# Merging two layers' attention loops of neighbouring batch elements in a decode kernel

## The chip, the cores and the metric

The kernel runs on one core of a Trainium2 chip. The metric is the device time of one execution in microseconds (us). *Slow* is a run over 1.5% above the fastest of the same kernel, and only *fast* runs enter the ratios.

Names used below: PE is the matmul engine (TensorE) and PEld its weight load, DVE is VectorE, ACT is ScalarE, POOL is GpSimd. "Issue" in the profile is time in which an engine waited for nothing that the profile shows. A "q spread" is the small group of PE matmuls that spreads a query out before its scores; it marks the same place in every element. A "packet" is one record of a DMA transfer in the trace.

## The reference

Two transformer-like layers with the same weights and the same K/V cache, one after the other: 4 batch elements, one token each, 32 query heads on 8 K/V heads, 4096 cached positions of 128 values, all bf16.

```python
B, Sq, D = 4, 1, 512;  Hq, Hkv, Sk, Dh = 32, 8, 4096, 128;  F = 1792   # cut
def _A_ref(x, k_cache, v_cache, wq, wo):
    q = (x @ wq).reshape(B, Sq, Hq, Dh)                    # transposes cut
    scores = einsum("bhqd,bhkd->bhqk", q, k) * Dh ** -0.5
    p = softmax(scores)
    return einsum("bhqk,bhkd->bhqd", p, v).reshape(B, Sq, Hq * Dh) @ wo
def _B_ref(x, w_gate, w_up, w_down):
    return (gelu(x @ w_gate) * (x @ w_up)) @ w_down

x = x + _A_ref(layernorm(x), ...)
x = x + _B_ref(layernorm(x), ...)
x = x + _A_ref(layernorm(x), ...)
x = x + _B_ref(layernorm(x), ...)
```

K and V are 33.5 MB each. The kernel keeps one element's transposed K on the chip for both layers, but reads V twice, so with the weights it moves 114.6 MB.

## The kernel before

Every K or V tile is a load of 512 KB into a ring of seven buffers, all issued from one engine. An element's K, V and V again are 48 such loads.

```python
KV_BUFS = 7
def load_kv(cache, b, kvh, t, name):
    tl = kvin.tile([P, CH, Dh], BF16, name=name, tag="kv")
    src = cache[b, kvh].rearrange("(p c) d -> p c d", p=P)
    dq.dma_start(out=tl[:], in_=src[:, t * CH:(t + 1) * CH])
    return tl

def turn(b, kvh):            # load K and transpose it with VectorE
    ...
        kn = load_kv(A_k_cache, b, kvh, t, "k_t")
        ...
            nc.vector.transpose(out=kt[...], in_=kf[:, :, bb])

def scores_head(sc, s, kvh, qb):          # 32 matmuls a head
    ...
            nc.tensor.matmul(sc[:, s, g, :], lhsT=kt[:, g, be // 2, :, be % 2],
                             rhs=qb[:, be, kvh]..., ...)

def soft_a(sc):              # max, exp
    nc.vector.tensor_reduce(out=colmax[:], in_=v, axis=AX.X, op=ALU.max)
    nc.gpsimd.partition_all_reduce(gmax..., colmax..., P, RED.max)
    nc.vector.tensor_tensor(out=w, in0=w, in1=gmax..., op=ALU.subtract)
    nc.scalar.activation(out=raw..., in_=sc..., func=ACT.Exp, scale=scale)

def soft_b(raw, pool):       # the "swap": 16 small matmuls, then a copy
    ...
            nc.tensor.matmul(x[a * QS:(a + 1) * QS, :, :, cc, :],
                             lhsT=ident_bf[:, cc * QS:(cc + 1) * QS], rhs=raw[:, :, :, a, :], ...)
    nc.scalar.copy(out=pe..., in_=x...)

def soft_c(pe):              # denominators with a matmul of ones
    nc.tensor.matmul(d..., lhsT=ones_bf[:, :], rhs=pe..., start=True, stop=True)
    nc.vector.tensor_reduce(out=den[:], in_=d..., axis=AX.X, op=ALU.add)

class Values:                # one step = one load of V and its 16 matmuls
    def step(self, count=1):
        ...
            v = load_kv(A_v_cache, self.b, kvh, t, "v_t")
            for i in range(CH):
                c = t * CH + i
                nc.tensor.matmul(self.ot[:], lhsT=v[:, i, :], rhs=pe[:, s, c, :],
                                 start=(c == 0), stop=(c == C - 1))

for b in range(B):
    for g in range(NG):                      # first layer, 4 groups of 2 heads
        ... turn, scores_head, soft_a, values of the group before, soft_b, soft_c, out_proj
    ... out_proj, norm, FFN, norm, q          # filled with second-layer values of element b-1
    for g in range(NG):                      # second-layer scores, on their own
        for s in range(GH):
            scores_head(sc, s, g * GH + s, qb2)
        nxt = soft_a(sc)
        ...
    prev = Values(b, 2, prob2)               # its values fill the next element's FFN
```

Of the kernel before, what the change touches and what calls it, by code (L numbers as in the profile page):

```python
# [8 lines left out]
FP32 = mybir.dt.float32  # L9
# [6 lines left out]
P = 128  # L16
# [4 lines left out]
GH = 2  # L21
QD = 4
QS = P // QD
KV_BUFS = 7
# [3 lines left out]
def kernel(  # L28
# [27 lines left out]
    NB = 2  # L56
# [9 lines left out]
    qbp = ctx.enter_context(tc.tile_pool(name="qbp", bufs=1))  # L66
    rawp = ctx.enter_context(tc.tile_pool(name="rawp", bufs=2))
    p1p = ctx.enter_context(tc.tile_pool(name="p1p", bufs=2))
    p2p = ctx.enter_context(tc.tile_pool(name="p2p", bufs=NG + 1))
    grp = ctx.enter_context(tc.tile_pool(name="grp", bufs=2 * NG))  # L70
    small = ctx.enter_context(tc.tile_pool(name="small", bufs=1))
    ps_sc = ctx.enter_context(tc.tile_pool(name="ps_sc", bufs=2, space=bass.MemoryType.PSUM))
    ps_ot = ctx.enter_context(tc.tile_pool(name="ps_ot", bufs=1, space=bass.MemoryType.PSUM))
    ps_y = ctx.enter_context(tc.tile_pool(name="ps_y", bufs=1, space=bass.MemoryType.PSUM))
    ps_x = ctx.enter_context(tc.tile_pool(name="ps_x", bufs=2, space=bass.MemoryType.PSUM))
# [6 lines left out]
    ones_bf = const.tile([P, P], BF16, name="ones_bf")  # L82
    nc.vector.memset(ones_bf[:], 1.0)
# [18 lines left out]
    wq_dram = A_wq.rearrange("(k p) n -> p k n", p=P)  # L102

# [21 lines left out]
    def ln_stats(b0, nb):  # L125
        bs = slice(b0, b0 + nb)
        st = ps_misc.tile([P, 2, nb, KD], FP32, name="st", tag="misc")
        nc.tensor.matmul(st[:], lhsT=mean_f[:, :], rhs=XX[:, :, bs], start=True, stop=True)
        return st

    def ln_apply(b0, nb, st):
        mv = small.tile([P, 2, nb], FP32, name="mv", tag="mv")
        nc.vector.tensor_reduce(out=mv[:], in_=st[:], axis=AX.X, op=ALU.add)
        msq = small.tile([P, nb], FP32, name="msq", tag="msq")
# [17 lines left out]
        for i in range(nb):  # L152
            nc.vector.tensor_scalar(out=xn_bf[:, :, b0 + i], in0=XX[:, 0, b0 + i],  # L153
                                    scalar1=mv[:, 0, i:i + 1], scalar2=rstd[:, i:i + 1],
                                    op0=ALU.subtract, op1=ALU.mult)

    def q_proj(b0, nb, h0, hp, dst):
        bs = slice(b0, b0 + nb)
        qps = ps_misc.tile([P, hp, nb], FP32, name="qps", tag="misc")
        for i in range(hp):  # L160
            m = h0 + i
            for k in range(KD):
                nc.tensor.matmul(qps[:, i, :], lhsT=wq_sb[:, k, m * Dh:(m + 1) * Dh],  # L163
                                 rhs=xn_bf[:, k, bs], start=(k == 0), stop=(k == KD - 1))
        nc.vector.tensor_copy(out=dst, in_=qps[:])

    def q_spread(q_rows, qb, h0, hp):
        qe = ps_misc.tile([P, NB * 2, hp], FP32, name="qe", tag="misc")
        for b in range(NB):
            for e in range(2):  # L170
                nc.tensor.matmul(qe[:, b * 2 + e], lhsT=sel[:, b, e].rearrange("p a i -> p (a i)"),
                                 rhs=q_rows, start=True, stop=True)
        k0, nk = h0 // rep, hp // rep
        for be in range(NB * 2):
            nc.vector.tensor_tensor(
                out=qb[:, be, k0:k0 + nk],
                in0=qe[:, be].rearrange("p (k h) -> p k h", h=rep).unsqueeze(2)
                    .broadcast_to([P, nk, QD, rep]),
                in1=amask[:].unsqueeze(1).unsqueeze(3).broadcast_to([P, nk, QD, rep]),
                op=ALU.mult)  # L180
# [23 lines left out]
    def gelu(nb, hg):  # L204
        sq = small.tile([P, KF, nb], FP32, name="sq", tag="sq")
        nc.scalar.activation(out=sq[:], in_=hg[:], func=ACT.Square)
        nc.vector.tensor_scalar(out=sq[:], in0=sq[:], scalar1=0.044715, scalar2=1.0,
                                op0=ALU.mult, op1=ALU.add)
        nc.vector.tensor_tensor(out=sq[:], in0=sq[:], in1=hg[:], op=ALU.mult)
        th = small.tile([P, KF, nb], FP32, name="th", tag="th")  # L210
        nc.scalar.activation(out=th[:], in_=sq[:], func=ACT.Tanh, scale=GELU_C)
        nc.vector.scalar_tensor_tensor(out=th[:], in0=th[:], scalar=1.0, in1=hg[:],
                                       op0=ALU.add, op1=ALU.mult)
        return th

    def gate_up(nb, th, hu):
        H_bf = small.tile([P, KF, nb], BF16, name="H_bf", tag="H_bf")
        nc.vector.scalar_tensor_tensor(out=H_bf[:], in0=hu[:], scalar=0.5, in1=th[:],
                                       op0=ALU.mult, op1=ALU.mult)
# [13 lines left out]
    def turn(b, kvh):  # L233
        kt = ktp.tile([P, G8, NB, QD, QS], FP32, name="kt", tag="kt")
        KT[kvh] = kt
        gt = CH // QD
        for t in range(NT):
            kn = load_kv(A_k_cache, b, kvh, t, "k_t")
            kf = kn.rearrange("p c d -> p (c d)").bitcast(FP32).rearrange(
                "p (c b i) -> p c b i", b=NB, i=QS)  # L240
            for bb in range(NB):
                nc.vector.transpose(  # L242
                    out=kt[:, t * gt:(t + 1) * gt, bb].rearrange("p g c j -> p g (c j)"),
                    in_=kf[:, :, bb])

    def scores_head(sc, s, kvh, qb):
        kt = KT[kvh].rearrange("p g b c j -> p (g b c j)").bitcast(BF16).rearrange(
            "p (g b m e) -> p g b m e", b=NB, m=P, e=2)
        for g in range(G8):
            for be in range(NB * 2):  # L250
                nc.tensor.matmul(sc[:, s, g, :], lhsT=kt[:, g, be // 2, :, be % 2],  # L251
                                 rhs=qb[:, be, kvh].rearrange("p a h -> p (a h)"),
                                 start=(be == 0), stop=(be == NB * 2 - 1))
# [4 lines left out]
    def soft_a(sc):  # L258
        v = sc.rearrange("p s g (a h) -> p s h (g a)", h=rep)
        colmax = grp.tile([P, GH, rep], FP32, name="colmax", tag="colmax", bufs=2)  # L260
        nc.vector.tensor_reduce(out=colmax[:], in_=v, axis=AX.X, op=ALU.max)  # L261
        gmax = grp.tile([P, GH, rep], FP32, name="gmax", tag="gmax", bufs=2)
        nc.gpsimd.partition_all_reduce(gmax.rearrange("p s h -> p (s h)"),  # L263
                                       colmax.rearrange("p s h -> p (s h)"), P, RED.max)
        w = sc.rearrange("p s g (a h) -> p s (g a) h", h=rep)
# [8 lines left out]
    def soft_b(raw, pool):  # L274
# [12 lines left out]
    def soft_c(pe):  # L287
        d = ps_x.tile([P, GH, C, rep], FP32, name="d", tag="x")
        nc.tensor.matmul(d.rearrange("p s c h -> p (s c h)"), lhsT=ones_bf[:, :],  # L289
                         rhs=pe.rearrange("p s c h -> p (s c h)"), start=True, stop=True)  # L290
        den = grp.tile([P, GH, rep], FP32, name="den", tag="den", bufs=2)
        nc.vector.tensor_reduce(out=den[:], in_=d.rearrange("p s c h -> p s h c"),  # L292
                                axis=AX.X, op=ALU.add)
        rden = grp.tile([P, GH, rep], FP32, name="rden", tag="rden")
        nc.vector.reciprocal(out=rden[:], in_=den[:])
        return rden

    class Values:
        def __init__(self, b, layer, prob):
            self.b, self.layer, self.prob, self.n = b, layer, prob, 0  # L300

        def step(self, count=1):
            for _ in range(count):
# [4 lines left out]
                pe, rden = self.prob[kvh // GH]  # L308
                s = kvh % GH
                if t == 0:  # L310
                    self.ot = ps_ot.tile([P, rep], FP32, name="ot", tag="ot")
                v = load_kv(A_v_cache, self.b, kvh, t, "v_t")
                for i in range(CH):
                    c = t * CH + i
                    nc.tensor.matmul(self.ot[:], lhsT=v[:, i, :], rhs=pe[:, s, c, :],  # L315
                                     start=(c == 0), stop=(c == C - 1))
                if t == NT - 1:
                    hs = slice(kvh * rep, (kvh + 1) * rep)
                    o = OT_bf[:, hs] if self.layer == 1 else OT2_bf[:, hs, self.b]
                    nc.vector.tensor_tensor(out=o, in0=self.ot[:], in1=rden[:, s], op=ALU.mult)  # L320
# [12 lines left out]
    ln_apply(0, B, ln_stats(0, B))  # L333

    prev = None
    for b in range(B):
        qb = qbp.tile([P, NB * 2, Hkv, QD, rep], BF16, name="qb", tag="qb")
        if b > 0:
            q_spread(q1_bf[:, :, b], qb, 0, Hq)
        prob = {}  # L340
        vals = Values(b, 1, prob)
        for g in range(NG):
            sc = new_scores()
            for s in range(GH):
                turn(b, g * GH + s)
                if b == 0 and s == 0:
                    q_proj(0, B, g * HG, HG, q1_bf[:, g * HG:(g + 1) * HG])
                    q_spread(q1_bf[:, g * HG:(g + 1) * HG, 0], qb, g * HG, HG)
                scores_head(sc, s, g * GH + s, qb)
            if b == 0 and g == 0:  # L350
                dq.dma_start(out=wq_sb[:, :, hq0:], in_=wq_dram[:, :, hq0:])
            raw = soft_a(sc)
            if g > 0:
                vals.step(GH * NT)
            pe = soft_b(raw, p1p)
            prob[g] = (pe, soft_c(pe))
            if b == 0 and g == 1:
                dq.dma_start(out=wo_sb[:], in_=A_wo.rearrange("(i p) n -> p i n", p=P))
            if g == 1:
                y1 = ps_y.tile([P, 1, KD], FP32, name="y1", tag="y")  # L360
            if g > 0:
                out_proj(y1, OT_bf, (g - 1) * HG, HG, g == 1, False)
        if b == 0:
            dq.dma_start(out=wg_sb[:], in_=B_w_gate.rearrange("(k p) n -> p k n", p=P))
        vals.step(GH * NT)
        if b == 0:
# [102 lines left out]
```

## Time and profile before

| quantity | before | where it is read |
|---|---|---|
| time, median of 3 (range) | 401.38 us (400.96 to 404.48) | runs |
| profiled run: span | 396.4 us | page |
| one element (start of a q spread to the next) | 85.2 and 82.3 us | PE timeline: 110.65, 195.86 and 278.15 |
| busiest: load queue, PE, DVE | 78%, 57%, 43% | page |
| stops of PE marked "issue", over 0.3 us | 9, together 9.8 us | PE timeline |

The page's chain that ended last, by engine and by line:

```profile
PE 31%; DVE 29%; DMA 26%; issue 8%; ACT 4%; POOL 2%; SPq 0%; POOLq 0%; ACTq 0%
DMA v_t<-in_A_v_cache_dram 16%; DVE kt L242 15%; PE sc L251 9%; PE ot L315 6%; DMA wd_sb<-in_B_w_down_dram 5%; DMA k_t<-in_A_k_cache_dram 4%; PE qps L163 3%; PE d L289 3%; ACT pe L283 2%; PE y L226 2%; DVE sc L266 2%; DVE colmax L261 2%; DVE den L292 2%; PE hg L200 2%; POOL gmax L263 2%
```

The page's groups of instructions (line, engine, operation, out<-in, shapes, count; then busy us and mean ns of one; then idle time before them and what ended most of it):

```profile
L251 PE MATMUL sc<-qb,kt 128*128 128x16 bf16 x2048 | 77.9, 175 | 37.8 <-DVE kt L242 32.5
...
L315 PE MATMUL ot<-pe,v_t 128*128 128x4 bf16 x2048 | 70.1, 166 | 34.7 <-DMA v_t<-in_A_v_cache_dram 19.2
...
L242 DVE STREAM_TRANSPOSE kt<-k_t 128x512 f32<-128x512 f32 x128 | 77.8, 674 | 9.4 <-DMA k_t<-in_A_k_cache_dram 9.4
...
L289 PE MATMUL d<-pe,ones_bf 128*128 128x256 bf16 x32 | 11.9, 372 | 27.8 <-ACT pe L283 27.8
...
L263 POOL PARTITION_ALL_REDUCE gmax<-colmax x32 | 11.8, 368 | 337.8 <-DVE colmax L261 337.8
```

A matmul's 166 ns is the length of its record; the records overlap, and the cadence is shorter. The PE timeline of before (start us, duration us, group, and in brackets the idle time before it with what ended it) shows it, in the second-layer scores of element 2:

```profile
259.27 1.62 PE L251 MATMUL sc<-qb,kt 128*128 128x16 bf16 x46
261.76 0.62 PE L251 MATMUL sc<-qb,kt 128*128 128x16 bf16 x18 [0.87 <-issue]
262.24 0.57 PE L315 MATMUL ot<-pe,v_t 128*128 128x4 bf16 x16
262.67 1.85 PE L251 MATMUL sc<-qb,kt 128*128 128x16 bf16 x64
264.37 0.57 PE L315 MATMUL ot<-pe,v_t 128*128 128x4 bf16 x16
264.87 0.40 PE L278 MATMUL x<-raw,ident_bf 128*32 128x64 bf16 x14
266.59 0.24 PE L278 MATMUL x<-raw,ident_bf 128*32 128x64 bf16 x2 [1.32 <-issue]
```

64 score matmuls start at 262.67 and the next group at 264.37: about 27 ns each.

### The profile page before, as it was taken

The page shows a single profiled execution, that of the slowest core. Times are in us where ns is not written, and L with a number is a line of the kernel's source. Part 1 is how long each engine was busy: PE and PEld are TensorE (multiplying, and loading weights), DVE is VectorE, ACT ScalarE, POOL GpSimd, SP SyncE. Part 2 cuts the span into 40 slices and gives each one's busy share as a digit, 9 for nine tenths or more (in the row PEclk, how much of TensorE's full clock was granted, in tenths as well). Part 3 has the DMA queues.
Part 4 walks back from the last instruction along what each step waited for, and adds up shares of the span by engine and source line. Part 5 has one row for each costly group of instructions (what it writes and reads, how often), then busy time and mean ns, then how long its engine had stood idle before and what let it go on. Part 6 is the DMA issues. An engine that isn't in the chain of part 4 may idle for free.

```text
span 396.4 us, 14928 instructions
## 1 busy us (share of the span) xinstructions
PE 227.7 (57%) x6848; PEld 206.1 (52%) x6848; DVE 172.3 (43%) x569; ACT 26.4 (7%) x75; POOL 12.5 (3%) x38
## 2 busy tenths in 40 slices
PE   0334266358445667667546667776456667767455
PEld 0323265357433556666435566766345566766344
DVE  0853364223376662233466563333766632232022
ACT  0020000000101000001100000011000000011000
POOL 0000000000100000001000000000000000010000
DMA  7999999992036999975578999974869999755920
GB/s 259 425 364 328 397 417 416 400 398 81 2 106 224 394 418 416 354 255 181 176 251 265 413 419 415 347 258 125 256 228 396 418 413 347 245 196 161 380 112 2
DMA packets 35759, 115.53 MB, mean 291 GB/s; under 512 B 3176, under 2 KB 9072, under 8 KB 35696
## 3 DMA queue, kind: packets, MB, share of 16 engines
q1 hardware_dynamic: 35696, 114.58, 77.9%
q8 instruction: 53, 0.87, 0.9%
q14 instruction: 10, 0.08, 0.1%
HBM read 114.56 MB, written 0.00 MB: 289 GB/s over the span
## 4 chain that ended last, share of the span: by engine, by line
PE 31%; DVE 29%; DMA 26%; issue 8%; ACT 4%; POOL 2%; SPq 0%; POOLq 0%; ACTq 0%
DMA v_t<-in_A_v_cache_dram 16%; DVE kt L242 15%; PE sc L251 9%; PE ot L315 6%; DMA wd_sb<-in_B_w_down_dram 5%; DMA k_t<-in_A_k_cache_dram 4%; PE qps L163 3%; PE d L289 3%; ACT pe L283 2%; PE y L226 2%; DVE sc L266 2%; DVE colmax L261 2%; DVE den L292 2%; PE hg L200 2%; POOL gmax L263 2%
## 5 line engine op out<-in xcount | busy, mean ns | idle before, releaser
L251 PEld LDWEIGHTS <-kt 128*128 128x128 bf16 x2048 | 67.3, 105 | 62.2 <-DVE kt L242 41.4
L251 PE MATMUL sc<-qb,kt 128*128 128x16 bf16 x2048 | 77.9, 175 | 37.8 <-DVE kt L242 32.5
L315 PE MATMUL ot<-pe,v_t 128*128 128x4 bf16 x2048 | 70.1, 166 | 34.7 <-DMA v_t<-in_A_v_cache_dram 19.2
L315 PEld LDWEIGHTS <-v_t 128*128 128x128 bf16 x2048 | 64.5, 105 | 43.9 <-DMA v_t<-in_A_v_cache_dram 23.0
L242 DVE STREAM_TRANSPOSE kt<-k_t 128x512 f32<-128x512 f32 x128 | 77.8, 674 | 9.4 <-DMA k_t<-in_A_k_cache_dram 9.4
L320 DVE TENSOR_TENSOR OT_bf<-ot,rden 128x4 bf16<-128x4 f32 x64 | 10.2, 159 | 53.4 <-PE ot L315 53.4
L292 DVE TENSOR_REDUCE den<-d 128x8 f32<-128x256 f32 x32 | 13.6, 425 | 39.1 <-PE d L289 39.1
L270 ACT ACTIVATE raw<-sc 128x256 bf16<-128x256 f32 x32 | 12.3, 384 | 242.7 <-DVE sc L266 123.9
L186 PEld LDWEIGHTS <-wo_sb 128*128 128x128 bf16 x640 | 19.9, 105 | 15.8 <-DMA wo_sb<-in_A_wo_dram 9.7
L289 PE MATMUL d<-pe,ones_bf 128*128 128x256 bf16 x32 | 11.9, 372 | 27.8 <-ACT pe L283 27.8
L261 DVE TENSOR_REDUCE colmax<-sc 128x8 f32<-128x256 f32 x32 | 13.6, 425 | 28.8 <-PE sc L251 28.8
L263 POOL PARTITION_ALL_REDUCE gmax<-colmax x32 | 11.8, 368 | 337.8 <-DVE colmax L261 337.8
L163 PE MATMUL qps<-xn_bf,wq_sb 128*128 128x1 bf16 (+1 forms) x640 | 18.7, 165 | 5.8 <-DVE xn_bf L153 5.8
L266 DVE TENSOR_TENSOR sc<-sc,gmax 128x256 f32<-128x256 f32 x32 | 13.8, 433 | 18.5 <-POOL gmax L263 18.5
L186 PE MATMUL y<-OT_bf,wo_sb 128*128 128x1 bf16 x512 | 16.4, 166 | 8.9 <-DMA wo_sb<-in_A_wo_dram 8.9
L163 PEld LDWEIGHTS <-wq_sb 128*128 128x128 bf16 x640 | 18.0, 104 | 6.5 <-issue 3.8
L278 PE MATMUL x<-raw,ident_bf 128*32 128x64 bf16 x512 | 13.2, 239 | 10.9 <-ACT raw L270 9.6
L278 PEld LDWEIGHTS <-ident_bf 128*32 128x32 bf16 x512 | 8.4, 118 | 13.6 <-issue 13.1
L200 PE MATMUL hg<-xn_bf,wg_sb 128*128 128x1 bf16 (+1 forms) x280 | 8.2, 165 | 11.6 <-DVE xn_bf L153 11.6
L200 PEld LDWEIGHTS <-wg_sb 128*128 128x128 bf16 x280 | 8.4, 105 | 12.0 <-issue 12.0
L283 ACT CAST pe<-x 128x256 bf16<-128x256 f32 x32 | 11.9, 370 | 22.8 <-PE x L278 22.8
L226 PE MATMUL y<-H_bf,wd_sb 128*128 128x1 bf16 (+1 forms) x280 | 8.6, 166 | 5.8 <-issue 4.0
(49 smaller groups left out, 103.2 us busy)
## 6 DMA issues: line engine op xcount, KB each, us to landing
v_t<-in_A_v_cache_dram SPq DMA_DIRECT2D x128, 512.0 KB, 7.2
k_t<-in_A_k_cache_dram SPq DMA_DIRECT2D x64, 512.0 KB, 6.9
wo_sb<-in_A_wo_dram SPq DMA_DIRECT2D x1, 4096.0 KB
wq_sb<-in_A_wq_dram SPq DMA_DIRECT2D x1, 3072.0 KB, 15.7
wg_sb<-in_B_w_gate_dram SPq DMA_DIRECT2D x1, 1792.0 KB
wu_sb<-in_B_w_up_dram SPq DMA_DIRECT2D x1, 1792.0 KB, 14.5
wd_sb<-in_B_w_down_dram SPq DMA_DIRECT2D x1, 1792.0 KB, 18.4
wq_sb<-in_A_wq_dram SPq DMA_DIRECT2D x1, 1024.0 KB, 5.2
```

The source lines that it names most:

```text
L163: nc.tensor.matmul(qps[:, i, :], lhsT=wq_sb[:, k, m * Dh:(m + 1) * Dh], rhs=xn_bf[:, k, bs], start=(k == 0), stop=(k == KD - 1))
L186: nc.tensor.matmul(y[:, :, dk], lhsT=wo_sb[:, i, dk * P:(dk + 1) * P], rhs=rhs, start=(first and i == h0 and dk == 0), stop=(last and i == ...
L200: nc.tensor.matmul(h[:, m, :], lhsT=w_sb[:, k, m * P:(m + 1) * P], rhs=xn_bf[:, k, bs], start=(k == 0), stop=(k == KD - 1))
L242: nc.vector.transpose(out=kt[:, t * gt:(t + 1) * gt, bb].rearrange("p g c j -> p g (c j)"), in_=kf[:, :, bb])
L251: nc.tensor.matmul(sc[:, s, g, :], lhsT=kt[:, g, be // 2, :, be % 2], rhs=qb[:, be, kvh].rearrange("p a h -> p (a h)"), start=(be == 0), s ...
L261: nc.vector.tensor_reduce(out=colmax[:], in_=v, axis=AX.X, op=ALU.max)
L266: nc.vector.tensor_tensor(out=w, in0=w, in1=gmax[:].unsqueeze(2).broadcast_to([P, GH, G8 * QD, rep]), op=ALU.subtract)
L278: nc.tensor.matmul(x[a * QS:(a + 1) * QS, :, :, cc, :], lhsT=ident_bf[:, cc * QS:(cc + 1) * QS], rhs=raw[:, :, :, a, :], start=True, stop= ...
L283: nc.scalar.copy(out=pe.rearrange("p s c h -> p (s c h)"), in_=x.rearrange("p s g c h -> p (s g c h)"))
L289: nc.tensor.matmul(d.rearrange("p s c h -> p (s c h)"), lhsT=ones_bf[:, :], rhs=pe.rearrange("p s c h -> p (s c h)"), start=True, stop=True)
L292: nc.vector.tensor_reduce(out=den[:], in_=d.rearrange("p s c h -> p s h c"), axis=AX.X, op=ALU.add)
L315: nc.tensor.matmul(self.ot[:], lhsT=v[:, i, :], rhs=pe[:, s, c, :], start=(c == 0), stop=(c == C - 1))
```

## The change

The intent is to remove the stage of second-layer scores, in which few loads run, by merging it into the next element's first-layer loop, which is full of loads. With it come smaller changes: K and V loads alternate; the denominator is summed on VectorE and POOL instead of with a ones-matmul; the whole second-layer value output collects in one PSUM bank and is scaled once; and the layer norm's `rstd` no longer scales the matmul's input but its output, so that the matmuls need not wait for it.

```diff
-        for i in range(nb):
-            nc.vector.tensor_scalar(out=xn_bf[:, :, b0 + i], in0=XX[:, 0, b0 + i],
-                                    scalar1=mv[:, 0, i:i + 1], scalar2=rstd[:, i:i + 1],
-                                    op0=ALU.subtract, op1=ALU.mult)
+        nc.vector.tensor_tensor(out=xn_bf[...], in0=XX[:, 0, bs], in1=mv[:, 0]..., op=ALU.subtract)
 ...
+    def q_norm(qps, dst, rstd, hp, nb):
+        nc.vector.tensor_tensor(out=dst, in0=qps[:], in1=spread_rstd(rstd, hp, nb), op=ALU.mult)
 ...
-    def soft_c(pe):
-        nc.tensor.matmul(d..., lhsT=ones_bf[:, :], rhs=pe..., start=True, stop=True)
-        nc.vector.tensor_reduce(out=den[:], in_=d..., axis=AX.X, op=ALU.add)
+    def soft_sum(raw):
+        nc.vector.tensor_reduce(out=cs[:], in_=raw..., axis=AX.X, op=ALU.add)
+        nc.gpsimd.partition_all_reduce(den..., cs..., P, RED.add)
 ...
+    def attend(b2, qb2, b1, qb1, rstd1):      # layer 2 of b2 with layer 1 of b1
+        for g in range(NG + 1):
+            if two and more:
+                sc2 = new_scores()
+                scores_head(sc2, 0, old[g * GH], g * GH, qb2)
+            if raw1 is not None:
+                prob1[g - 1] = soft_swap(raw1, p1p)
+            turn()                            # one K load, two transposes
+            if raw1 is not None:
+                den1 = soft_sum(raw1)
+            if two and more:
+                scores_head(sc2, 1, old[g * GH + 1], g * GH + 1, qb2)
+                gm2 = soft_max(sc2)
+            if g > 0:
+                vals.step()                   # one V load, 16 matmuls
+            turn()
 ...                                          # four turns and four value steps in all
+            if more:
+                sc1 = new_scores()
+                for s in range(GH):
+                    scores_head(sc1, s, KT[g * GH + s], g * GH + s, qb1)
+                gm1 = soft_max(sc1)
 ...
-        for g in range(NG):
-            sc = new_scores()
-            for s in range(GH):
-                scores_head(sc, s, g * GH + s, qb2)
-            nxt = soft_a(sc)
 ...
+            y1, prob2, rden2 = attend(b, qb2, b + 1, qb1, None)
```

## The prediction

> **What bounds the kernel now.** No engine: the page shows PE busy 57%, VectorE 43%, the load queue's DMA 78%. It is a row of stages with different limits. The slices show 413-419 GB/s in some stretches and 80-260 in others. [...] this trace peaks near 418. 114.6 MB at 418 is about 274 us (estimate), so some 120 of the 396 us are lost to slower stretches.
>
> From the timeline, elements 1-3 take about 82 us each (query spread at 195.9 and again at 278.2). Of these, 41 us is the first layer: 8 transposes (4.75 us per group), then the serial softmax (max 0.43, POOL 0.38, subtract 0.43, exp 0.38, swap, copy 0.37, ones-matmul 0.37, sum 0.43). About 19 us is FFN and q projection, filled with second-layer values. About 18.5 us is second-layer scores, with few loads and no transposes. An element's K, V, V are 48 loads of 512 KB, 60.4 us at peak. In the chain of waits, transposes take 15%, value DMA 16%, score matmuls 9%.
>
> **What the change does.**
> - Second-layer scores of element b go into the first-layer loop of b+1: the 18.5 us stretch disappears, three times. Its PE work (256 matmuls, about 7.2 us at the timeline's 28 ns cadence) and VectorE softmax (about 5 us) go under the loop's 40 us of loads.
> - K and V loads alternate, so loads flow evenly.
> - The denominator comes from raw on VectorE plus a second POOL all-reduce: the ones-matmul (32 x 0.37 us) and the swap-copy-matmul-sum delay leave the chain; POOL gains 32 x 0.37. [...] I expect the POOL times to stay.
> - rstd leaves the path into hg and q: 11 VectorE steps, 2.2 us per norm, run beside matmuls, for one more multiply of 0.2.
> - Waits of PE for value scaling (15.2 us in the view of waits) go; the query spread is one VectorE instruction instead of four or eight.
>
> **Sum (estimates from those durations).**
> - Element 0's first layer stays DMA-bound: 30.7 MB landed by about 84 us; then the whole output projection (3.6) and an unfilled FFN: 103 us.
> - Merged iteration: VectorE 7.9 us busy, dependence loop about 9.7, DMA 8 loads = 10.1. First and last iterations 10.2 and 4.5. FFN stage 19-21 against 20.1 of loads. Period about 65 us (floor 60.4), three times = 195.
> - Last element's second layer: 22. Final FFN and output: 12.5 (13.2 now).
>
> Span about 332; the measured time is some 3 us above it: **335 us**, range 320 to 352. Faster by over 2%: 0.97; same 0.02; slower 0.01.
>
> **What would show it.** DMA above 380 GB/s in most slices from 105 to 290 us; no second-layer scores without transposes; period 63-68 us; the chain led by value and K loads, transposes beside them; 64 POOL all-reduces of about 0.37 us; no d matmul; transposes still 0.67 us by name.
>
> **What would make it wrong.** The loop's dependences ([...] one swap bank, seven load buffers) stall DMA: period 70+. POOL slowed beside VectorE. PE fetch gaps ("issue", 0.9-1.4 us today) multiply. [...] The late weights ahead of element 0's last values delay it. If buffers absorb everything, period 61 and time near 320.

The sum is 103 + 3 x 65 + 22 + 12.5 = 332.5 us of span, and some 3 us more make the 335. The 418 GB/s in it are the rate in the stretches of full loads on the page of before; one slice there has 425.

## More of the kernel before

The page of the kernel before: busy time of two engines; then rows in 40 slices of the span (tenths of busy time, and GB/s moved); then the DMA queues (packets, MB, share of 16 engines).

```profile
span 396.4 us, 14928 instructions
PE 227.7 (57%) x6848; PEld 206.1 (52%) x6848; DVE 172.3 (43%) x569; ACT 26.4 (7%) x75; POOL 12.5 (3%) x38
...
PE   0334266358445667667546667776456667767455
...
DMA  7999999992036999975578999974869999755920
GB/s 259 425 364 328 397 417 416 400 398 81 2 106 224 394 418 416 354 255 181 176 251 265 413 419 415 347 258 125 256 228 396 418 413 347 245 196 161 380 112 2
...
q1 hardware_dynamic: 35696, 114.58, 77.9%
q8 instruction: 53, 0.87, 0.9%
```

The loads run at 413 to 419 GB/s in some stretches and at 125 to 260 in others, while no engine is near full.

## The result, and the profile after

| | before | after |
|---|---|---|
| median (range), us | 401.47 (400.96 to 404.48), 4 runs | 373.79 (369.32 to 375.1), 4 runs |
| ratio of fast runs | 1 | 0.9266, 95% interval 0.9181 to 0.9351 |

A ratio here is the mean time of one kernel's fast runs over that of the other's of the same rounds, so it is not quite the ratio of the medians. The change is 28 us faster where 66 us were predicted, and the time lies outside the predicted range.

The profiled run of these four was slow (375.1 us). The lines below are therefore from a fast run of the same kernel in the first experiment, the control e1_after_again (span 366.8 us); the profiled slow run had the same pattern (22 stops of PE marked "issue", together 43.3 us, against 23 and 37.3 in the control).

The page of the changed kernel, the same rows as before:

```profile
span 366.8 us, 14915 instructions
PE 204.7 (56%) x6848; PEld 193.5 (53%) x6848; DVE 160.3 (44%) x502; ACT 26.4 (7%) x70; POOL 25.1 (7%) x70
...
PE   0344240428846466865565747665575575867755
...
DMA  7999999997067999999789999998799899992930
GB/s 237 420 417 388 411 379 413 403 397 294 4 220 250 342 371 353 384 358 361 265 262 369 375 325 361 369 338 289 262 363 321 280 378 412 321 347 92 340 123 2
...
q1 hardware_dynamic: 36240, 114.58, 85.3%
q8 instruction: 53, 0.87, 0.9%
```

The loads are more even, as intended, but from 110 to 293 us (slices 13 to 32) they run at 250 to 384 GB/s: a single one of these twenty slices is above the 380 that was predicted for most.

The chain that ended last, in the changed kernel:

```profile
PE 39%; DMA 29%; DVE 15%; issue 14%; POOL 1%; ACT 1%; SPq 0%; ACTq 0%; POOLq 0%; DVEq 0%
DMA v_t<-in_A_v_cache_dram 29%; PE sc L266 12%; PE ot L334 10%; DVE kt L254 7%; PE qps L166 3%; PE y L190 3%; DVE colmax L273 2%; PE y L232 2%; PE hg L204 2%; PE x L293 2%; PE hu L204 2%; PE st L128 1%; DVE sc L281 1%; POOL gmax L275 1%; PE yf L190 1%
```

VectorE's share of the chain halved, from 29% to 15%. PE's share and "issue" grew. The groups of the changed kernel:

```profile
L334 PE MATMUL ot<-pe,v_t 128*128 128x4 bf16 x2048 | 69.1, 166 | 75.6 <-DMA v_t<-in_A_v_cache_dram 58.7
...
L254 DVE STREAM_TRANSPOSE kt<-k_t 128x512 f32<-128x512 f32 x128 | 82.8, 685 | 26.3 <-DMA k_t<-in_A_k_cache_dram 14.8
L266 PE MATMUL sc<-qb,kt 128*128 128x16 bf16 x2048 | 62.9, 174 | 12.9 <-issue 8.9
...
L275 POOL PARTITION_ALL_REDUCE gmax<-colmax x32 | 11.9, 371 | 225.7 <-DVE colmax L273 144.3
...
L307 POOL PARTITION_ALL_REDUCE den<-cs x32 | 12.7, 398 | 84.7 <-DVE cs L304 84.7
...
L304 DVE TENSOR_REDUCE cs<-raw 128x8 f32<-128x256 bf16 x32 | 12.4, 389 | 4.2 <-ACT raw L285 4.2
```

The score matmuls no longer wait 32.5 us for transposes; what ends most of their idle time now is "issue". The value matmuls wait 58.7 us for their loads, three times as long as before. None of the operations shown became more than 2% slower: transposes 674 to 685 ns, the old all-reduce 368 to 371 ns; the new one takes 398 ns.

The PE timeline of the changed kernel, in the stage after the first merged loop, shows what "issue" looks like:

```profile
155.94 0.27 PE L334 MATMUL ot<-pe,v_t 128*128 128x4 bf16 x5
158.58 0.86 PE L334 MATMUL ot<-pe,v_t 128*128 128x4 bf16 x27 [2.37 <-issue]
159.31 1.63 PE L232 MATMUL y<-H_bf,wd_sb 128*128 128x1 bf16 x56
160.80 0.99 PE L334 MATMUL ot<-pe,v_t 128*128 128x4 bf16 x32
161.65 0.57 PE L128 MATMUL st<-XX,mean_f 128*128 128x8 f32 x2
162.08 0.43 PE L334 MATMUL ot<-pe,v_t 128*128 128x4 bf16 x11
163.03 0.72 PE L334 MATMUL ot<-pe,v_t 128*128 128x4 bf16 x21 [0.52 <-issue]
```

PE stops in the middle of 32 value matmuls whose data is there (the first 5 of them had started), and again in the middle of a group. Between the two stops lie 27 + 56 + 32 + 2 + 11 = 128 matmuls, again 256 instructions. The stops fall on a fixed count of instructions and not on a tile's edge.

Where the 35 us of span against the predicted 332 lie, read from the start of the first merged loop's scores (98.98 us), of the q spread in that loop and the next two (100.69, 176.58, 252.12 us) and, for the third period, of the first FFN matmuls (227.9 and 305.7 us):

| part | predicted us | measured us | difference |
|---|---|---|---|
| up to element 1 | 103 | about 99 | -4 |
| three periods | 3 x 65 = 195 | 75.9 + 75.5 + 77.8 = 229 | +34 |
| last second layer and final part | 34.5 | about 39 | +4 |

So the missing gain is in the periods. In the first two periods the stops marked "issue" add up to 11.3 and 13.0 us, in before's two periods to 3.5 and 2.2 us. That their sum is about the miss of a period (10.7 us) is not yet a proof: a stop costs nothing where PE would have waited anyhow.

**The theory.** PE's instructions are loaded too, in blocks of 256: the trace has 53 packets of 16,384 bytes each on q8, whose time the page gives as a share of the same 16 DMA engines as that of the loads (0.9% and 85.3%), and between two stops lie 256 PE instructions. The guess is that with the engines full of loads a block takes longer to arrive than PE needs to work through one, and that PE runs dry. Whether the blocks cost time is what the experiments ask; without loads it will turn out that they do not (e3, no stop), under full loads that they do (e4, 28 stops of 43.2 us).

**The rivals.** (a) The ring of seven buffers and the dependences of the merged loop hold back loads, and PE waits for them; the stops hide behind these waits. (b) Something else in the change (denominators on POOL, `rstd` after the matmuls, four merged iterations of too much work) lengthened the period.

### The profile page after: what moved, and what is told of

It reads as the page before. It is cut to its first block, busy times and chain, and to the rows that moved or that the text cites. A ratio compares the mean times of both kernels' runs of the same rounds, so it can differ in the third digit from the quotient of the medians.

```text
span 373.3 us, 14915 instructions
## 1 busy us (share of the span) xinstructions
PE 204.4 (55%) x6848; PEld 193.2 (52%) x6848; DVE 160.4 (43%) x502; ACT 26.5 (7%) x70; POOL 25.1 (7%) x70
## 4 chain that ended last, share of the span: by engine, by line
PE 38%; DMA 29%; issue 16%; DVE 15%; POOL 1%; ACT 1%; SPq 0%; ACTq 0%; POOLq 0%; DVEq 0%
DMA v_t<-in_A_v_cache_dram 29%; PE sc L266 11%; PE ot L334 10%; DVE kt L254 7%; PE qps L166 3%; PE y L190 3%; DVE colmax L273 2%; PE y L232 2%; PE hg L204 2%; PE hu L204 2%; PE x L293 1%; PE st L128 1%; DVE sc L281 1%; POOL gmax L275 1%; PE yf L190 1%
## 5 line engine op out<-in xcount | busy, mean ns | idle before, releaser
L254 DVE STREAM_TRANSPOSE kt<-k_t 128x512 f32<-128x512 f32 x128 | 82.8, 686 | 26.9 <-DMA k_t<-in_A_k_cache_dram 16.8
L266 PE MATMUL sc<-qb,kt 128*128 128x16 bf16 x2048 | 63.0, 175 | 17.5 <-issue 13.6
L266 PEld LDWEIGHTS <-kt 128*128 128x128 bf16 x2048 | 58.9, 104 | 20.0 <-issue 15.2
L166 PE MATMUL qps<-xn_bf,wq_sb 128*128 128x1 bf16 (+1 forms) x640 | 20.2, 166 | 11.3 <-issue 10.1
L293 PEld LDWEIGHTS <-ident_bf 128*32 128x32 bf16 x512 | 9.8, 118 | 31.6 <-issue 30.9
L166 PEld LDWEIGHTS <-wq_sb 128*128 128x128 bf16 x640 | 18.9, 104 | 11.8 <-issue 11.2
L307 POOL PARTITION_ALL_REDUCE den<-cs x32 | 12.7, 398 | 85.7 <-DVE cs L304 85.7
L338 DVE TENSOR_TENSOR OT_bf<-ot,rden 128x8 bf16<-128x8 f32 (+1 forms) x23 | 3.5, 153 | 33.7 <-PE ot L334 33.7
L281 DVE TENSOR_TENSOR sc<-sc,gmax 128x256 f32<-128x256 f32 x32 | 13.5, 422 | 8.9 <-POOL gmax L275 8.7
L304 DVE TENSOR_REDUCE cs<-raw 128x8 f32<-128x256 bf16 x32 | 12.4, 389 | 3.8 <-ACT raw L285 3.8
L171 DVE TENSOR_TENSOR q_bf<-qps,rstd 128x8 bf16<-128x8 f32 (+1 forms) x20 | 3.3, 170 | 24.0 <-PE qps L166 23.6
L179 DVE TENSOR_TENSOR qb<-qe,amask 128x128 bf16<-128x128 f32 (+1 forms) x23 | 7.8, 338 | 5.6 <-PE qe L177 5.5
## 6 DMA issues: line engine op xcount, KB each, us to landing
wo_sb<-in_A_wo_dram SPq DMA_DIRECT2D x2, 2048.0 KB, 12.5
```

Source lines behind the costliest of these rows:

```text
L166: nc.tensor.matmul(qps[:, i, :], lhsT=wq_sb[:, k, m * Dh:(m + 1) * Dh], rhs=xn_bf[:, k, bs], start=(k == 0), stop=(k == KD - 1))
L254: nc.vector.transpose(out=self.kt[:, t * gt:(t + 1) * gt, bb].rearrange("p g c j -> p g (c j)"), in_=kf[:, :, bb])
L281: nc.vector.tensor_tensor(out=w, in0=w, in1=gmax[:].unsqueeze(2).broadcast_to([P, GH, G8 * QD, rep]), op=ALU.subtract)
L293: nc.tensor.matmul(x[a * QS:(a + 1) * QS, :, :, cc, :], lhsT=ident_bf[:, cc * QS:(cc + 1) * QS], rhs=raw[:, :, :, a, :], start=True, stop= ...
L304: nc.vector.tensor_reduce(out=cs[:], in_=raw.rearrange("p s g a h -> p s h (g a)"), axis=AX.X, op=ALU.add)
L307: nc.gpsimd.partition_all_reduce(den.rearrange("p s h -> p (s h)"), cs.rearrange("p s h -> p (s h)"), P, RED.add)
```

## The experiments

Several kernels below are wrong: they use the wrong K or V, or leave values out. The comparison cannot tell whether the attention is right, and it is weak evidence for the variants meant to be right as well.

Times are medians with ranges where a kernel was timed in rounds. "Period" is the time from one q spread to the next in the profiled run. "Stops" are the PE stops over 0.3 us marked "issue".

### e1_after_again: the control

The changed kernel without an edit.

> Control: the changed kernel again, beside the runs that follow. Both theories: 369 to 375 us, about 20 stops of PE of over 0.3 us with nothing to wait for (fetch of instructions), some 43 us together, and a period of 74 to 79 us from one second-layer query projection's end to the next.

Measured: 369.13 us (366.48 to 376.28), ratio 0.9185 (0.9126 to 0.9243), periods 75.9 and 75.5, 23 stops of 37.3 us in all. Its lines are shown above.

### e2_five_bufs: fewer loads in flight through a smaller ring

```diff
-KV_BUFS = 7
+KV_BUFS = 5
```

> Five load buffers instead of seven, so at most five loads are outstanding. Fetch theory (PE's instruction packets queue behind the outstanding loads): the stops get shorter, under 28 us together instead of 43, while a shallower prefetch costs some of it: 362 to 378 us. Ring theory (loads are issued in one fixed order, each when the buffer seven loads back is free, so too few buffers starve PE and VectorE): stops stay near 43 us, waits for values grow, over 382 us.

Measured: 414.02 us (408.13 to 415.88; two of the four runs were slow, the fast ones took 408.1 and 412.5), ratio 1.0234 (1.0139 to 1.033). The stops shrink to 15 with 20.6 us, as they should if loads in flight delay the instructions, but PE's wait for `v_t` grows to 127.6 us (the profiled run was a slow one). Fewer buffers cost more prefetch than they spare in stops. The stops came out as the fetch theory expected and the time (over 382 us) as the ring theory did; neither is decided: the ring matters in this kernel.

### e3_resident and e4_traffic: loads that nobody waits for

The ring can be taken out altogether. In e3 one K/V tile is loaded once and used for everything (wrong). In e4 the same tile is used, and all loads of K and V are issued as well, into six buffers that nobody reads.

```diff
+    RES = {}
     def load_kv(cache, b, kvh, t, name):
+        if not RES:                                   # e3 and e4
+            RES[0] = state.tile([P, CH, Dh], BF16, name="kv_res")
+            ...                                       # one load
+        tl = kvin.tile(...)                           # e4 only
+        dq.dma_start(out=tl[:], in_=src[...])         # e4 only
+        return RES[0]
```

> Wrong result on purpose: one K/V tile is loaded once and every transpose and value matmul reads it, so nothing but weights is loaded. Fetch theory: with the DMA engines idle the stops nearly vanish after the weights have landed (under 6 us together for elements 1 to 3), period 58 to 64 us. If the stops stay at 10 us a period, fetch is slow by itself, not because of loads. Ring theory: the same period without loads, 58 to 64 us, but the stops were not its cause and may stay.

> Wrong result on purpose: as the resident kernel, but all K and V loads are still issued, into six buffers that nobody reads, so the DMA engines are as full as before while no compute instruction waits for a load. Fetch theory: PE's stops come back, 8 to 14 us a period while the traffic lasts (until about 275 us), period 68 to 76 us. Ring theory: the period stays within 2 us of the resident kernel's, because no one waits for the ring.

Measured: e3 276.66 us, periods 57.9 and 57.9, no stop at all. e4 335.79 us, periods 74.9 and 72.9, 28 stops of 43.2 us in all. PE's instructions and all dependences among the engines are those of e3. The PE timeline of e3, in the stage of the FFN of element 1:

```profile
115.33 1.63 PE L207 MATMUL hu<-xn_bf,wu_sb 128*128 128x1 bf16 x56
116.82 0.99 PE L337 MATMUL ot<-pe,kv_res 128*128 128x4 bf16 x32
117.68 1.63 PE L235 MATMUL y<-H_bf,wd_sb 128*128 128x1 bf16 x56
119.17 0.99 PE L337 MATMUL ot<-pe,kv_res 128*128 128x4 bf16 x32
```

The same stage in the PE timeline of e4:

```profile
140.76 1.63 PE L210 MATMUL hu<-xn_bf,wu_sb 128*128 128x1 bf16 x56
142.26 0.27 PE L340 MATMUL ot<-pe,kv_res 128*128 128x4 bf16 x5
144.90 0.86 PE L340 MATMUL ot<-pe,kv_res 128*128 128x4 bf16 x27 [2.37 <-issue]
145.62 1.63 PE L238 MATMUL y<-H_bf,wd_sb 128*128 128x1 bf16 x56
147.11 0.99 PE L340 MATMUL ot<-pe,kv_res 128*128 128x4 bf16 x32
147.96 0.57 PE L134 MATMUL st<-XX,mean_f 128*128 128x8 f32 x2
148.39 0.43 PE L340 MATMUL ot<-pe,kv_res 128*128 128x4 bf16 x11
150.71 0.72 PE L340 MATMUL ot<-pe,kv_res 128*128 128x4 bf16 x21 [1.89 <-issue]
```

The stop sits after the same 5 value matmuls as in the real kernel, and the next after 128 more. Two rows of e4's page, in 40 slices, show how full the engines are:

```profile
PE   0245657214676566756378476674665656899985
...
GB/s 234 399 417 413 381 409 377 415 400 396 415 418 416 416 416 415 411 409 416 416 416 416 397 409 382 413 417 414 412 390 399 417 414 417 174 6 4 4 4 2
```

Loads run near 415 GB/s until about 285 us and then end. Up to there PE is mostly busy 5 to 7 tenths of a slice, and after it 8 to 9. Intervals between the starts of instruction packets, worked out from the trace's record of queue q8 (us):

```
e4, while the loads last (from 6.48):  6.48 5.85 5.92 6.03 5.93 5.70 5.94 6.05 5.85 5.86 5.92 5.88 5.93 5.85 5.94 6.05 ... 5.97 5.80 6.00 5.94
e4, after the last load:               3.39 3.48 3.88 3.47 3.76 3.94 3.40 3.53 3.74 3.50
e3, no loads:                          3.3 to 5.9 in the periods, twice 8.4 to 8.6
```

With the engines full a block comes every 5.9 us (5.70 to 6.48 in the two periods), whatever the stage does. 128 matmuls at 28 ns need 3.6. The time without loads falls as low as 3.3, and there it is PE that sets the pace. A period has about 3,200 PE instructions, counted between two q spreads, which is 12.5 blocks; 12.5 x 5.93 = 74 us, and e4's mean is 73.9. That is longer than the 60.4 us that the loads of a period need. The product by itself is bookkeeping: blocks times their mean interval give the period in any kernel, in e3 with 4.6 us. What counts is that the interval hardly moves from 5.9 us while the work changes.

The trace ties each stop to a packet, in the real kernels too. This is worked out from the starts and durations of q8's packets and from PE's instructions, semaphore instructions counted. Each of the 9 stops of before, the 23 of the control and the 28 of e4 ends 1.2 to 1.6 us after a packet has landed, and the number of instructions done by then is 256 times the packets landed, plus 193 or 194, every time; the stops of the other runs below do the same. PE stops where the instructions that have landed end.

The same records show which part of the way grows (medians in the first two periods). A packet is not moved more slowly: it takes 1.0 us in e3 and 0.9 in e4. It starts later: 0.5 us after PE has entered the block that the packet before it brought in e3, 3.6 us in e4. With 0.9 us for the move and 1.4 us until PE goes on, that is 5.9 us. So 5.93 us is the delay of one block, repeated: in e4's two periods no packet starts before PE has entered the block of the one before, as if one block were fetched at a time.

The delay costs 16 us a period though nobody waits for a load. In e4's two periods the stops are 16.2 and 17.6 us, and PE's other waits are no longer than in e3. The same instructions and the same dependences without that traffic take 57.9 us, so rival (b) falls with e3, and rival (a) cannot explain e4, where PE waits for no buffer. It does not say how much of the real kernel's period is fetch alone, since there PE's stops and the ring act on each other: the control's first two periods hold 11.3 and 13.0 us of stops and 7.9 and 6.7 us of waits for `v_t`, where e3 has neither.

### f1_traffic_depth3 and f2_traffic_2kb: what delays a block

In f1 each load of e4 also waits for the load three before it, so that at most three are outstanding. In f2 each load is cut in two, with 2 KB instead of 4 KB for each partition.

```diff
# f1
+        ld = dq.dma_start(...)
+        if len(LOADS) >= 3:
+            tc.add_manual_dep(ld.ins, LOADS[-3].ins.name, ...)      # a real wait
# f2
+        for h in range(0, CH, CH // 2):
+            dq.dma_start(out=tl[:, h:h + CH // 2], in_=src[:, t * CH + h:...])
```

> Wrong result on purpose: the traffic kernel, but each load is issued only when the load three before it has landed (three outstanding instead of six). In the traffic kernel one packet of 256 PE instructions arrived every 5.9 us while the loads ran, and 3.4 to 3.9 us after they ended. If the packet waits behind all outstanding loads, the interval falls to 4 to 4.8 us and the period from 74 to 60-65 us. If a packet's delay is set by the sharing of the engines alone, the interval stays at 5.6 to 6 us and the period at 72 to 75 us.

> Wrong result on purpose: the traffic kernel with each load cut into two of 2 KB per partition. If the packet waits its turn behind whole pieces of the loads, smaller pieces shorten the interval: 3.5 to 5 us, period 60 to 68 us. If it waits behind bytes, 5.6 to 6.2 us and 72 to 76 us.

Measured: f1 401.75 us, periods 66.5 and 67.4, packets on average 5.4 us apart and irregular, 28 stops of 37.2 us. The total grew because the loads slowed: the row of f1's page is

```profile
GB/s 255 341 347 265 362 245 342 343 332 331 283 303 291 292 272 272 288 304 281 268 297 268 278 288 279 299 254 280 278 284 273 295 279 291 272 287 275 285 283 239
```

f2 took 344.12 us, periods 72.1 and 69.9, packets about 5.7 us apart, 31 stops of 46.4 us. Neither run fits either of the two cases that were expected of it in full: f1's interval and period and f2's period lie between them. With half the piece (64,032 packets of loads on q1 instead of 36,384) a block still came only after 5.7 us, against 5.9. Fewer outstanding loads and smaller pieces each help a little: a packet starts 2.6 us (f1) and 3.2 us (f2) after PE has entered the block before, against 3.6. But both edits also lowered the rate of the loads (the row above; 300 to 400 GB/s in most slices of f2), so what shortened the wait is not separated, and neither is the lever. What the packet waits behind stays open.

### f3_depth3 and f4_depth2: the same limit in the real kernel

The edit of f1, in the changed kernel itself; f4 with two loads instead of three.

> The changed kernel with seven buffers, but at most three loads outstanding. Fetch theory with a delay that grows with the outstanding loads: stops fall from 37-43 us to under 20 us, 345 to 362 us. Fetch theory with a fixed delay: stops as before and some prefetch lost, 368 to 380 us. Ring theory: nothing gained, 368 to 380 us.

> The same with at most two outstanding[...]. With a delay that grows with the outstanding loads: stops under 12 us, but DMA below 400 GB/s in its best slices; 345 to 370 us. With a fixed delay: stops as before, 375 to 395 us.

Measured: f3 426.46 us (423.47 to 429.6), ratio 1.0653 (1.0553 to 1.0752), periods 85.0 and 90.1; f4 506.85 us (503.54 to 510.94), ratio 1.2632 (1.2524 to 1.274). Both times lie far outside everything that was expected (at most 380 and 395 us). The stops nearly vanish, 8 with 11.4 us and 3 with 3.5 us. But the loads slow down (270 and 227 GB/s on average, against 315 in the control), and PE waits for `v_t` 145.7 and 229.8 us. Stops go away when the engines are not full, which fits the theory but does not test it, since a PE that waits for values also needs its next block later; and a kernel that lives on its loads cannot pay for it that way.

### g1_half_values and k1_traffic_half: fewer instructions

Every second value matmul is left out (wrong): 1,024 matmuls and their weight loads in all, 45 packets instead of 53, 10.5 instead of 12.5 in a period. All loads stay. g1 is the real kernel, k1 is e4.

```diff
-                for i in range(CH):
+                for i in range(0, CH, 2):
```

> Wrong result on purpose: every second value matmul is left out (2048 PE instructions of 13668 fewer, two packets of 256 a period), loads and waits unchanged. Fetch theory: with the DMA engines full a packet needs 5.9 us, so a period of some 12.5 packets (74 us) becomes 10.5 (62 us, just above the 60.4 us of loads): 335 to 350 us. If PE's instructions are not what binds (the resident kernel had a period of 57.9 us with all of them, below the loads' 60.4), 358 to 369 us.

> Wrong result on purpose: the traffic kernel without every second value matmul, 10.5 packets a period instead of 12.5. The traffic kernel had 73.9 us for 12.5 packets and 80.1 us for 13.5. If its period is packets times 5.9 us, it is now 61 to 64 us; the real kernel with the same cut had 69, and what is above 62 there is then waiting for loads. If the period doesn't follow the packets, it is 70 us or more here too.

Measured: g1 347.88 us (347.24 to 348.64), ratio 0.8693 (0.8649 to 0.8737), periods 69.6 and 68.6, 13 stops of 21.9 us. k1 311.68 us, periods 63.2 and 62.8, packets 5.9 us apart; 10.5 x 5.93 = 62.3. With nobody waiting for loads, the period follows the number of blocks. In the real kernel, g1 missed the 62 us of the pure count by about 7; since k1 has the same instructions and the same loads and takes 63, the 6 us between them come with PE's waits for loads (11.8 and 10.0 us on `v_t` in g1's two periods, none in k1). g1 alone would not decide anything: the work that it takes from PE, 256 matmuls a period at 28 ns, is 7 us too, as much as the period fell. (The expectation counts 13,668 PE instructions; the page of the changed kernel has 6,848 matmuls and as many weight loads, 13,696.)

### j1_resident_more, j2_traffic_more, j3_more: more instructions

The reverse: 1,024 weight loads that nobody uses, one after every second value matmul, one more block in a period. j1 is e3, j2 is e4, and j3 is the real kernel.

```diff
+                    if i % 2:
+                        nc.tensor.ldweights(ident_bf[:, :])
```

> Wrong result on purpose: the resident kernel (nothing loaded but weights) with 1024 weight loads on PE that no matmul uses, one after every second value matmul: 256 PE instructions, one packet, more a period. Both theories: with the DMA engines idle they cost at most their own time on PE[...], so the period goes from 57.9 to at most 62 us, with no stops of over 0.3 us for fetch.

> Wrong result on purpose: the same 1024 weight loads in the traffic kernel. Fetch theory: one packet more a period at 5.9 us: 73 to 75 us become 79 to 82 us. If the instructions only cost PE time: as much more as the resident kernel showed, and less than 4 us.

> Correct result: the changed kernel with the same 1024 idle weight loads, four packets in all. No engine's useful work and no wait is changed. Fetch theory: 10 to 22 us slower than the changed kernel (366 to 374): 378 to 394 us. If the number of instructions doesn't bind: within 4 us of it, 366 to 377 us.

Measured: j1 310.22 us, period 66.1, one stop. It missed what was expected: 256 bare weight loads added 8.2 us to a period, 32 ns each, more than I had taken them to cost. That spoils j3 as a test: 383.98 us (380.17 to 388.24), ratio 0.9586 (0.9504 to 0.9669), in the expected range but explained by PE work as well as by fetch. j2 is still of use: 360.7 us, periods 79.2 and 80.9, packets again 5.9 us apart. Under full loads the addition cost 6.2 us a period, one block, less than the 8.2 us that the same instructions cost with no loads. So PE's added work went, for the most part, into the time that PE spends waiting for blocks.

In the three kernels with traffic the interval stays at 5.9 to 6.0 us, whatever the work, and the period follows the number of blocks:

| kernel | blocks in a period | blocks x 5.93 us | mean period measured |
|---|---|---|---|
| k1_traffic_half | 10.5 | 62.3 | 63.0 |
| e4_traffic | 12.5 | 74.1 | 73.9 |
| j2_traffic_more | 13.5 | 80.1 | 80.1 |

### g2_ones: the denominators back on PE

The ones-matmul of before instead of the sum on VectorE and POOL.

```diff
-    def soft_sum(raw):
-        nc.vector.tensor_reduce(out=cs[:], in_=raw..., op=ALU.add)
-        nc.gpsimd.partition_all_reduce(den..., cs..., P, RED.add)
+    def soft_sum(pe):
+        nc.tensor.matmul(d..., lhsT=ones_bf[:].broadcast_to([P, P]), rhs=pe..., start=True, stop=True)
+        nc.vector.tensor_reduce(out=den[:], in_=d..., axis=AX.X, op=ALU.add)
```

> One part undone: the denominators come again from a ones-matmul on the swapped values instead of VectorE's sum and POOL. The prediction's chain argument: the swap, copy, matmul, sum delay comes back into each iteration, 2 us or more in each, 378 us or more. Fetch theory: PE is held by its packets and only 32 matmuls come back, 369 to 376 us.

Measured: 374.28 us (369.06 to 378.35), ratio 0.9279 (0.9196 to 0.9361). That is the changed kernel's ratio (0.9185, 0.9253, 0.9266 in its three sets of rounds). Moving the denominators is neither the gain nor the loss: in the merged loop their chain runs beside something longer.

### g3_rstd_first: the scale back in front of the matmuls

```diff
-        nc.vector.tensor_tensor(out=xn_bf[...], in0=XX[...], in1=mv..., op=ALU.subtract)
+        ln_scale(b0, nb, mv)             # all steps of rstd, then (x - mean) * rstd
 ...
-        nc.vector.tensor_tensor(out=dst, in0=qps[:], in1=spread_rstd(rstd, hp, nb), op=ALU.mult)
+        nc.vector.tensor_copy(out=dst, in_=qps[:])
```

> One part undone: the reciprocal deviation scales xn before the matmuls again, so 11 VectorE steps (2.2 us) stand before hg and before the projection of q. As predicted, 1.5 to 2 us come back in each of nine norms: 381 us or more. Fetch theory: in the FFN stage PE waits for its packets most of the time, which hides part of it; only where the DMA engines idle (element 0 and the end) does all of it return: 371 to 378 us.

Measured: 374.76 us (373.12 to 376.26), ratio 0.9363 (0.9312 to 0.9414). Against the changed kernel's ratios that is 0.010 to 0.018, so about 4 to 7 us, not the 14 to 18 expected of the prediction's argument; the controls ran on other chips or in other rounds, and the interval of one of them overlaps. The FFN's first matmuls wait for `xn_bf` 2.62 us in element 0 and 3.15 us at the end, but only 0.35 to 0.99 us in elements 1 to 3, where value matmuls fill the time; the projections of q wait 2.53 us in element 0 and 0.46 to 1.68 us in elements 1 to 3. The part is worth most where nothing fills.

### h1_carry and h2_swap4: two attempts at a better kernel

h1 moves four of the 16 second-layer value steps from the FFN stage into the first iteration of the merged loop, which has no values of its own. h2 does the swap with 4 matmuls of 256 columns in place of 16, which takes 12 matmuls and 12 weight loads off each swap (50 packets instead of 53), and four ACT copies in place of one. To make room it also has one buffer instead of two for the first layer's swapped values and for their PSUM output, and a narrower matrix for the mean. h2_control is the changed kernel once more, on h2's chip and in its rounds.

```diff
# h1
             if g > 0:
                 vals.step()
+            elif carry is not None:
+                carry.step()             # four places; the FFN stage fills less
# h2
         for cc in range(QD):
-            for a in range(QD):
-                nc.tensor.matmul(x[a * QS:(a + 1) * QS, :, :, cc, :],
-                                 lhsT=ident_bf[:, cc * QS:(cc + 1) * QS], rhs=raw[:, :, :, a, :], ...)
+            nc.tensor.matmul(x[:, cc]..., lhsT=spread[:, cc]..., rhs=raw..., ...)
-        nc.scalar.copy(out=pe..., in_=x...)
+        for a in range(QD):
+            nc.scalar.copy(out=pe[rows]..., in_=x[rows, :, :, a, :])
```

> An improvement meant to spread PE instructions and loads: four of the sixteen second-layer value steps leave the FFN stage and fill the first iteration of the merged loop, which had only four loads in about 9.5 us. Fetch theory: the FFN stage has 128 PE instructions fewer (half a packet, 3 us) and a less full DMA, the first iteration has room: 355 to 365 us beside 369 to 374 of the changed kernel. If neither helps, 367 to 375 us.

> A correct kernel with fewer PE instructions and the same PE time: the swap of four partition blocks by four matmuls of 256 columns (each block repeated in all four places, and four ACT copies take the right one) instead of sixteen of 64 columns. 768 PE instructions fewer of 13668, three packets. Fetch theory: at the 10.6 ns an instruction that leaving out half the value matmuls gave, 6 to 10 us less than the changed kernel beside it, less what the longer copy (about 1.5 us instead of 0.37) gives back: 360 to 368 us. If the gain of that run came from less PE work and not from fewer instructions, this run gains nothing: 369 us or more.

> The changed kernel once more, on the same chip and in the same rounds as the run before it, for a comparison without the spread between chips: 366 to 376 us.

Measured: h1 373.81 us (368.01 to 376.75), ratio 0.9254 (0.9186 to 0.9323), the same as the changed kernel and not the 355 to 365 hoped for. h2 368.72 us (364.27 to 373.26), ratio 0.9141 (0.9076 to 0.9205), against 371.09 us (367.43 to 374.95), ratio 0.9253 (0.9196 to 0.931) of h2_control. h2 is about 1% better, in the direction of the theory, but just above the 360 to 368 expected; the intervals overlap and it is not a settled gain; the four wide swap matmuls take 1.0 us where the 16 narrow ones took 0.4, and the four copies 1.45 us where the one took 0.37. I have no version that clearly beats the changed kernel.

## Why the prediction was wrong

The direction was right and the size was not. The step that failed is "Period about 65 us (floor 60.4), three times = 195". The three periods took 229 us, 34 more, and that is nearly the whole miss of 35 us of span.

- **Where it failed.** The sum compared the loads (60.4 us) with chains of VectorE, POOL and PE at PE's cadence of 28 ns. It left out that PE's instructions are loads too. With the engines full of K and V, a block of 256 instructions comes every 5.93 us, so PE does 128 matmuls in 5.93 us, 46 ns each. A period's 12.5 blocks need 74 us then, more than the loads themselves. Shown by e3 against e4 (57.9 to 73.9 us), by the constant interval of k1, e4 and j2, and, in the changed kernel's own trace, by the 23 stops that all end just after a packet has landed.
- **Why before did not show it.** The old stages kept full loads and dense matmuls mostly apart: 9 stops, 9.8 us. Merging them is what the change is for, and so it brings the two together. The prediction had "PE fetch gaps ('issue', 0.9-1.4 us today) multiply" among its risks, without a number. The count could have been had: the 128 matmuls between two stops of before and the 53 packets on its page were in sight. The 5.93 us a block under full loads are a measurement of e4.
- **What the real kernel adds.** There PE's stops and the ring act on each other: a stopped PE gives back no buffer, so loads start later (their issuer waits 102.1 us for value matmuls in the changed kernel's profiled run, which was slow, and 78.4 in before's; slices of 262 to 289 GB/s in the page after), and then PE waits for `v_t` (58.7 us against 19.2). The fetch alone makes 73.9 us (e4), the real kernel has 75.7; with half the values 63 against 69. How much of the real period each would cause alone is not separated, since no run could take the fetch away and keep the loads that PE waits for.
- **The removal of the second-layer stage: right.** No scores of the second layer run without transposes except the last element's, and VectorE's share of the chain fell from 29% to 15%. A period fell from 83.8 to 75.7 us (means of two). Without fetch delay and loads, e3, it is 57.9: the merged dependences themselves fit below the floor of the loads. The risk that the loop's dependences would hold it is not what happened.
- **POOL: right.** 64 all-reduces of 371 and 398 ns beside a busy VectorE. In the control six of the new all-reduces ran in part beside a `tensor_reduce` and took 397 to 398 ns, as those did beside which VectorE was idle.
- **Denominators and rstd: right in mechanism, oversized.** The ones-matmul is gone, and putting it back changes nothing measurable (g2). `rstd` is worth 4 to 7 us (g3), mostly in element 0 and at the end.
- **Value scaling: right.** The waits of value matmuls for the scaling of the bank (15.2 us in before's view of waits) are gone; what is left are 7.8 us before the output projection.
- **Load rate: wrong.** One slice of twenty above 380 GB/s. The peak was 425 GB/s in a slice before and 420 after.
- **The other terms.** Up to element 1: 103 predicted, 99 measured. Last second layer and final part: 34.5 and about 39; five of the 23 stops, together 9.7 us, come after 300 us.

## What to carry to other kernels

Before merging stages so that dense small matmuls run under full loads, count PE's instructions: take the time of one instruction block under full loads (here 5.93 us for 256 instructions, so 46 ns for a matmul with its weight load; it changed with the loads, to 5.4 and 5.7 us in f1 and f2), multiply, and compare with the loads' own time; in e4 the product was the larger, 74.1 us against 60.4, and the period was 73.9. In a trace, look for stops marked "issue" and count the matmuls between two of them: here it was 128, or a multiple, time after time, which pointed to the fetch and not to a dependence; that each stop ended just after a packet of instructions had landed (1.2 to 1.6 us) confirmed it. To test it, keep the traffic and take the waits away (loads into buffers that nobody reads): that one pair of runs decided what changing the depth, the ring or the work did not.
